# Re-cutting the HBM blocks of a streaming `x + gamma * y` kernel: 8, 60 and 60 rows instead of 4, 64 and 60

## The chip, the cores and the metric

The kernel runs on one core of a Trainium2 chip. The metric is the device time of one execution in microseconds, lower is better. Three runs of the kernel before gave 119.56, 119.86 and 119.68 us, median 119.68 us. A separate execution was profiled; its page and trace are what the rest of this document reads.

## The reference

```python
B, S, D = 1024, 16, 512          # x, y: bfloat16 [1024, 16, 512]; gamma: bfloat16 [512]
def reference(x, y, gamma):
    return x + gamma * y
```

Flattened, there are 16384 rows of 512 numbers (1024 bytes each). The core has 128 partitions, so each partition handles 128 rows. "A row" below means one such row in every partition at once: 128 x 1024 bytes, or 131072 bytes. x, y and the output have 128 rows each, 384 rows (50.33 MB) in all that must cross between HBM and the on-chip memory.

## The kernel before

Everything is written out by hand: which engine issues which transfer, which semaphore it waits for, and in which order the vector engine works. There are no loops over tiles at run time.

**Blocks.** `BLOCKS = [4, 64, 60]` cuts the 128 rows into three regions of HBM. In each region `rows_of` gives partition p one contiguous stretch of memory: 4, 64 or 60 rows of it. A transfer may cover part of one block, not parts of two.

**Transfers.** A transfer is written `(tensor, first row, end row[, slot])`; for x the slot is where it lands in `x_sb`, which holds only 76 rows, so later x loads overwrite rows of x that have been used up. y lands in `y_sb`, which holds all 128 rows; the results are written over y and stored from there. The queue of SyncE (SP) issues the list `SP`, the queue of ScalarE (ACT) issues the list `ACT`:

```python
SP  = [('y', 0, 4), ('y', 4, 68), ('x', 4, 68, 4), ('y', 68, 128), ('x', 68, 120, 24), ('x', 120, 128, 0)]
ACT = [('x', 0, 4, 0), ('g',), ('s', 4, 68), ('s', 0, 4), ('s', 68, 128)]
```

`'g'` loads gamma, `'s'` stores. In the text a transfer is called by its list entry, for instance "y 4:68" or "the store 68:128". Within one list the order is fixed, and an issuing queue that waits holds up all that is behind it.

**What holds transfers back.** `EARLY = (2, 1)` puts the first two SP transfers and the first ACT transfer ahead of the start-up barrier of the program. `HOLD = ('y', 0, 4)` with `AHEAD = (2, 1)`: the third SP transfer and the second ACT transfer wait until y 0:4 has landed; TensorE takes that semaphore and passes it on (L147, L149). `RELEASE = ('x', 68, 120, 24)`: no store is issued before that load has landed; again TensorE waits for it and passes it on, to ACT as `s_go` (L158) and to VectorE as `s_rel` (L159). An x load that overwrites rows in `x_sb` waits for the additions that read those rows (`frees`). A store waits for its additions through the counter `s_add`.

**Vector work.** `PIECES = [8, 16, 44, 52, 8]` cuts the rows for VectorE: piece 0 is rows 0:8, piece 1 is 8:24, piece 2 is 24:68, piece 3 is 68:120, piece 4 is 120:128. `('m', c)` multiplies piece c of y by gamma in place (L180), `('a', c)` adds x (L189). The order is

```python
DVE = [('m', 0), ('m', 1), ('m', 2), ('a', 2), ('a', 0), ('a', 1), ('m', 3), ('m', 4), ('a', 3), ('a', 4)]
```

Each operation waits for the loads that cover its piece. Gamma is copied to all partitions by one matmul with a row of ones (L152) and a copy out of PSUM (L154).

Of the kernel before, what the change touches and what calls it, by code (L numbers as in the profile page):

```python
# [3 lines left out]

BLOCKS = [4, 64, 60]

PIECES = [8, 16, 44, 52, 8]


SP = [
    ('y', 0, 4),
    ('y', 4, 68),
    ('x', 4, 68, 4),
    ('y', 68, 128),
    ('x', 68, 120, 24),
    ('x', 120, 128, 0),
]
ACT = [('x', 0, 4, 0), ('g',), ('s', 4, 68), ('s', 0, 4), ('s', 68, 128)]  # L20

EARLY = (2, 1)

HOLD, AHEAD = ('y', 0, 4), (2, 1)

RELEASE = ('x', 68, 120, 24)

DVE = [('m', 0), ('m', 1), ('m', 2), ('a', 2), ('a', 0), ('a', 1), ('m', 3), ('m', 4), ('a', 3), ('a', 4)]
MULT, ADD = mybir.AluOpType.mult, mybir.AluOpType.add


def _take(sem, n, eng):


    return eng.wait_ge(sem, n).then_inc(sem, -n)  # L35


def kernel(
# [18 lines left out]
    rows = N // P  # L57
    n = len(PIECES)
    assert sum(PIECES) == rows
    starts = [sum(PIECES[:c]) for c in range(n + 1)]  # L60
    dt = xf.dtype
    edges = [sum(BLOCKS[:c]) for c in range(len(BLOCKS) + 1)]
    assert edges[-1] == rows

    def rows_of(t, a, b):

        c = max(c for c in range(len(BLOCKS)) if edges[c] <= a)
        assert b <= edges[c + 1]
# [6 lines left out]
    y_sb = nc.alloc_sbuf_tensor("y_sb", [P, rows, D], dt).ap()  # L75
    x_loads = [w for w in ACT + SP if w[0] == "x"]
    y_loads = [w for w in SP + ACT if w[0] == "y"]
    stores = [w for w in SP + ACT if w[0] == "s"]
    for loads in (x_loads, y_loads, stores):
# [9 lines left out]
    s_add, s_go, s_rel, s_end, s_out = sem("s_add"), sem("s_go"), sem("s_rel"), sem("s_end"), sem("s_out")  # L89
    added = [a for kind, *a in DVE if kind == "a"]  # L90
    order = {a[0]: k for k, a in enumerate(added)}

    def meets(a, b, c, d):
        return a < d and c < b
# [4 lines left out]
    def x_at(row):  # L99
        return next(w[3] + row - w[1] for w in x_loads if w[1] <= row < w[2])  # L100
# [12 lines left out]
    def ring(eng, what, n_early, n_ahead):  # L113

        known, went = 0, False
        for k, w in enumerate(what):
            kind = w[0]
            if k == n_ahead:
                _take(s_held[eng], 1, eng)
            need = frees(w) if kind == "x" else pieces_of(w[1], w[2]) + list(w[3:]) if kind == "s" else []  # L120
            need = max((order[c] + 1 for c in need), default=0)
            if kind == "s" and not went:
                _take(s_go, 1, eng)
                went = True
            if need > known:
                eng.wait_ge(s_add, need)
                known = need
            if kind == "g":
                i = eng.dma_start(out=gamma_row, in_=gamma.unsqueeze(0)).then_inc(s_gamma, 16)
            elif kind == "x":  # L130
                to = x_sb[:, w[3] : w[3] + w[2] - w[1], :]
                i = eng.dma_start(out=to, in_=rows_of(xf, w[1], w[2])).then_inc(s_load[w], 16)
            elif kind == "y":
                r = slice(w[1], w[2])
                i = eng.dma_start(out=y_sb[:, r, :], in_=rows_of(yf, w[1], w[2])).then_inc(s_load[w], 16)
            else:
                r = slice(w[1], w[2])
                i = eng.dma_start(out=rows_of(of, w[1], w[2]), in_=y_sb[:, r, :]).then_inc(s_out, 16)
            if k < n_early:
                early.append(i.ins)  # L140

    ring(nc.sync, SP, EARLY[0], AHEAD[0])
    ring(nc.scalar, ACT, EARLY[1], AHEAD[1])

# [11 lines left out]

    _take(s_load[RELEASE], 16, nc.tensor)
    nc.tensor.sem_inc(s_go, 1)  # L158
# [4 lines left out]
    def need(loads, c):  # L163
        for w in loads:
            if w not in landed and meets(starts[c], starts[c + 1], w[1], w[2]):
                if w == RELEASE:
                    _take(s_rel, 1, nc.vector)
                elif w == HOLD:
                    _take(s_held[nc.vector], 1, nc.vector)
                else:  # L170
                    _take(s_load[w], 16, nc.vector)
                landed.add(w)

    for kind, *args in DVE:
        c = args[0]
        yt = y_sb[:, starts[c] : starts[c + 1], :]
        if kind == "m":
            need(y_loads, c)
            g = gamma_sb[:, None, :].to_broadcast([P, PIECES[c], D])
            nc.vector.tensor_tensor(out=yt, in0=yt, in1=g, op=MULT).then_inc(s_dve, 1)  # L180
            open_mults += 1
        else:
# [4 lines left out]
            at = x_at(starts[c])  # L187
            xt = x_sb[:, at : at + PIECES[c], :]
            nc.vector.tensor_tensor(out=yt, in0=xt, in1=yt, op=ADD).then_inc(s_add, 1)  # L189
# [44 lines left out]
```

## Time and profile before

| what | value |
|---|---|
| median of three runs | 119.68 us (119.56 to 119.86) |
| profiled execution, first to last instruction | 118.2 us |
| runs' median less that span | 1.5 us, lies around the span; the page gives no other time for the profiled execution |
| VectorE busy | 70.1 us (59%), 12 instructions |
| TensorE busy | 0.6 us |
| moved by DMA | 50.33 MB, mean 426 GB/s over the span |
| share of 16 DMA engines' span taken by packets | 64.8% SP's queue + 33.9% ACT's queue |

How to read it: `q1` is SP's DMA queue, `q10` is ACT's. Both feed the same 16 DMA engines. In the timeline a `DMA_DIRECT2D` row of SPq or ACTq is the issuing of a transfer, not the transfer; the list of DMA issues gives the time from issue to landing, so issue time plus that time is when the transfer's semaphore has reached its full count. The list leaves the size out where a partition's stretch is 64 rows. The profile's rows for VectorE name a tile by partitions x elements: 128x4096 is 8 rows, 128x8192 16 rows, 128x22528 44 rows, 128x26624 52 rows.

### The profile page before, as it was taken

To read this page: it belongs to the slowest core of one execution; us is meant where nothing else is said; L and a number is where in the kernel's file an instruction comes from. 1 tells how busy PE (TensorE), PEld (TensorE's weight loads), DVE (VectorE), ACT (ScalarE), POOL (GpSimd) and SP (SyncE) were. 2 spreads that over 40 slices of the span, in tenths; PEclk is the share of its full clock that TensorE was granted. 3 is DMA by queue.
4 is the path that set the end of the run, shared out by engine and by line. 5 is a ranking of instruction groups with operands and counts; after the bars stand their busy time and mean duration, and the time that the engine had idled before them with its cause. 6 is when DMAs were issued, how large, how long until landed. Compare 5 with 4: busy or idle time off the path is not lost. (4 is left out here: it accounts for less than half of the span.)

```text
span 118.2 us, 91 instructions
## 1 busy us (share of the span) xinstructions
PE 0.6 (0%) x1; PEld 0.1 (0%) x1; DVE 70.1 (59%) x12; POOL 0.2 (0%) x4
## 2 busy tenths in 40 slices
PE   0000100000000000000000000000000000000000
PEld 0000000000000000000000000000000000000000
DVE  0000200089999969999999999999999900000000
POOL 0000000000000000000000000000000000000000
DMA  6999889988899879879969696898899889799793
GB/s 248 461 666 399 355 355 399 665 355 355 355 599 466 355 333 624 374 333 499 499 288 576 288 576 288 360 637 355 355 576 488 355 355 510 333 582 416 333 499 166
DMA packets 1442, 50.33 MB, mean 426 GB/s; under 512 B 161, under 2 KB 162, under 8 KB 546
## 3 DMA queue, kind: packets, MB, share of 16 engines
q1 hardware_dynamic: 864, 33.03, 64.8%
q10 hardware_dynamic: 578, 17.30, 33.9%
HBM read 33.56 MB, written 16.78 MB: 426 GB/s over the span
## 5 line engine op out<-in xcount | busy, mean ns | idle before, releaser
L180 DVE TENSOR_TENSOR y_sb<-y_sb,gamma_sb 128x4096 bf16<-128x4096 bf16 (+3 forms) x5 | 34.7, 6981 | 10.9 <-DVEq L35 10.9
L189 DVE TENSOR_TENSOR y_sb<-x_sb,y_sb 128x4096 bf16<-128x4096 bf16 (+3 forms) x5 | 34.7, 6981 | 1.2 <-DVEq L35 1.1
L154 DVE CAST gamma_sb<-gamma_ps 128x512 bf16<-128x512 f32 x1 | 0.7, 692 | 10.2 <-DVEq L35 10.2
L146 DVE MEMSET ones_row<- 1x128 bf16 x1 | 0.2, 165 | 2.0 <-PEq L51 2.0
L152 PE MATMUL gamma_ps<-gamma_row,ones_row 1*128 1x512 bf16 x1 | 0.6, 581 | 11.6 <-PEq L35 11.6
L152 PEld LDWEIGHTS gamma_ps<-gamma_row,ones_row 1*128 1x128 bf16 x1 | 0.1, 101 | 11.6 <-issue 11.6
L218 POOL MEMSET const-bfloat16-1.0<- 128x1 bf16 x1 | 0.1, 101 | 0.0
L218 POOL MEMSET const-uint8-127<- 128x1 uint8 x1 | 0.1, 101 | 0.0
L218 POOL MEMSET const-float32-0.0<- 128x1 f32 x1 | 0.1, 98 | 0.2 <-issue 0.2
L218 POOL MEMSET const-float32-1.0<- 128x1 f32 x1 | 0.1, 98 | 0.0
## 6 DMA issues: line engine op xcount, KB each, us to landing
y_sb<-in_y_dram SPq DMA_DIRECT2D x1, 7680.0 KB, 57.3
out_dram<-y_sb ACTq DMA_DIRECT2D x1, 7680.0 KB, 23.8
x_sb<-in_x_dram SPq DMA_DIRECT2D x1, 6656.0 KB, 21.7
x_sb<-in_x_dram SPq DMA_DIRECT2D x1, 1024.0 KB, 22.0
y_sb<-in_y_dram SPq DMA_DIRECT2D x1, 512.0 KB, 3.4
x_sb<-in_x_dram ACTq DMA_DIRECT2D x1, 512.0 KB, 4.2
out_dram<-y_sb ACTq DMA_DIRECT2D x1, 512.0 KB, 22.3
y_sb<-in_y_dram SPq DMA_DIRECT2D x1, 23.4
```

Source lines behind the costliest of these rows:

```text
L146: nc.vector.memset(ones_row, 1.0).then_inc(s_ones, 1)
L152: nc.tensor.matmul(gamma_ps, ones_row, gamma_row, start=True, stop=True).then_inc(s_ps, 1)
L154: nc.vector.tensor_copy(out=gamma_sb, in_=gamma_ps).then_inc(s_dve, 1)
L180: nc.vector.tensor_tensor(out=yt, in0=yt, in1=g, op=MULT).then_inc(s_dve, 1)
L189: nc.vector.tensor_tensor(out=yt, in0=xt, in1=yt, op=ADD).then_inc(s_add, 1)
L218: nc = _bacc.Bacc("TRN2", target_bir_lowering=False, num_devices=1)
```

## The change

The blocks become 8, 60 and 60 rows. The head is the 8 rows of y alone, issued by SP; the head's 8 rows of x are the last load instead of the first. The x load 68:128 is one transfer, and piece 3 is 60 rows. ACT has no transfer ahead of the barrier; its first is gamma, behind the hold. The stores are 60, 60 and 8 rows, and the 8-row head is the last of them. The functions are unchanged.

```diff
-BLOCKS = [4, 64, 60]
-
-PIECES = [8, 16, 44, 52, 8]
+BLOCKS = [8, 60, 60]
+
+PIECES = [8, 16, 44, 60]
 
 
 SP = [
-    ('y', 0, 4),
-    ('y', 4, 68),
-    ('x', 4, 68, 4),
+    ('y', 0, 8),
+    ('y', 8, 68),
+    ('x', 8, 68, 0),
     ('y', 68, 128),
-    ('x', 68, 120, 24),
-    ('x', 120, 128, 0),
+    ('x', 68, 128, 16),
+    ('x', 0, 8, 0),
 ]
-ACT = [('x', 0, 4, 0), ('g',), ('s', 4, 68), ('s', 0, 4), ('s', 68, 128)]
-
-EARLY = (2, 1)
-
-HOLD, AHEAD = ('y', 0, 4), (2, 1)
-
-RELEASE = ('x', 68, 120, 24)
-
-DVE = [('m', 0), ('m', 1), ('m', 2), ('a', 2), ('a', 0), ('a', 1), ('m', 3), ('m', 4), ('a', 3), ('a', 4)]
+ACT = [('g',), ('s', 8, 68), ('s', 68, 128), ('s', 0, 8)]
+
+EARLY = (2, 0)
+
+HOLD, AHEAD = ('y', 0, 8), (2, 0)
+
+RELEASE = ('x', 68, 128, 16)
+
+DVE = [('m', 0), ('m', 1), ('m', 2), ('a', 2), ('a', 1), ('m', 3), ('a', 3), ('a', 0)]
```

## The prediction

> **What bounds the kernel now.** I read the page from the top. VectorE is busy 59% of the span, no other engine counts, and the chain of waits accounts for only 14% of the span, since it does not follow transfers. The queues account for the rest:
>
> ```profile
> ## 3 DMA queue, kind: packets, MB, share of 16 engines
> q1 hardware_dynamic: 864, 33.03, 64.8%
> q10 hardware_dynamic: 578, 17.30, 33.9%
> HBM read 33.56 MB, written 16.78 MB: 426 GB/s over the span
> ```
>
> 64.8% and 33.9% make 98.7%: of 118.2 us the sixteen DMA engines lack packets for 1.5 us. So the question is whether the transfers stand end to end. The DMA issues give the time to landing, the timeline the issue:
>
> ```profile
> y_sb<-in_y_dram SPq DMA_DIRECT2D x1, 7680.0 KB, 57.3
> out_dram<-y_sb ACTq DMA_DIRECT2D x1, 7680.0 KB, 23.8
> x_sb<-in_x_dram SPq DMA_DIRECT2D x1, 6656.0 KB, 21.7
> x_sb<-in_x_dram SPq DMA_DIRECT2D x1, 1024.0 KB, 22.0
> y_sb<-in_y_dram SPq DMA_DIRECT2D x1, 512.0 KB, 3.4
> x_sb<-in_x_dram ACTq DMA_DIRECT2D x1, 512.0 KB, 4.2
> out_dram<-y_sb ACTq DMA_DIRECT2D x1, 512.0 KB, 22.3
> y_sb<-in_y_dram SPq DMA_DIRECT2D x1, 23.4
> x_sb<-in_x_dram SPq DMA_DIRECT2D x1, 39.5
> ...
> out_dram<-y_sb ACTq DMA_DIRECT2D x1, 21.5
> ```
>
> ```profile
> 0.00 0.85 SPq L135 DMA_DIRECT2D y_sb<-in_y_dram  x2
> ...
> 3.71 0.33 SPq L132 DMA_DIRECT2D x_sb<-in_x_dram  x1
> 3.90 0.50 ACTq L129 DMA_DIRECT2D gamma_row<-in_gamma_dram  x1
> 4.09 0.43 SPq L135 DMA_DIRECT2D y_sb<-in_y_dram  x1
> ...
> 55.37 2.53 SPq L132 DMA_DIRECT2D x_sb<-in_x_dram  x2
> ...
> 77.41 17.36 ACTq L138 DMA_DIRECT2D out_dram<-y_sb  x3
> ```
>
> Rows merged here ("x2", "x3") start, singly, at 0.00 and 0.42; 55.37 and 57.58; 77.41, 77.81 and 94.43. Issue plus time to landing: y 0:4 at 3.4, x 0:4 at 4.3, y 4:68 at 0.42 + 23.4 = 23.8, x 4:68 at 43.2, y 68:128 at 61.4, x 68:120 at 77.1, x 120:128 at 79.6, stores at 98.9, 100.1 and 118.2. The steps are 19.4 us for 64 rows, 18.2 for 60, 15.7 for 52, 2.5 for 8, then 19.3, 1.2 and 18.1 for 64, 4 and 60 rows stored: 0.302 to 0.303 us a row in all the wide ones, loads and stores, and the narrow ones the same within rounding. Each step is the transfer's own bytes; none holds a pause. In the trace's packet records every engine starts the next transfer's first packet within 0.05 us of its last one of the transfer before. So no transfer waits for VectorE; I check below that this stays so.
>
> **The row transfers.** The bytes are the same: 384 rows. Ten row transfers become nine: y 0:4, x 0:4, y 64, x 64, y 60, x 52, x 8, and stores 64, 4, 60 give way to y 8, y 60, x 60, y 60, x 60, x 8, and stores 60, 60, 8. A transfer is 8 packets on each engine, one per partition. Their durations by size are 2.418 us (65536 bytes), 2.267 (61440), 0.309 (8192) and 0.159 (4096). From the two ends, (2.418 - 0.159) / 61440 bytes = 36.8 ns per 1000 bytes, which leaves 0.159 - 0.151 = 0.008 us a packet. One transfer fewer saves 8 x 0.008 = 0.06 us. Above, I can bound the cost of a transfer by stores 4 and 60 together, 1.2 + 18.1 = 19.3 us, against 19.3 us for the one of 64 rows: with 0.1 us rounding, 0 to 0.15. I take 0.07, the packet value; range 0 to -0.2 (the upper bound plus the slow first packets of the cold start: y 0:4 took 1.36 us an engine where the store of 4 rows took 1.27).
>
> Here the Trainium skill points elsewhere. "DMA: Bandwidth & Descriptors", section "Anatomy of one DMA", fits a fixed 2.0 us per DMA plus the bytes (for GpSimd's path); by it one transfer fewer would give about 117.7 us. The same page, "Measured (HBM→SBUF, 128 partitions, SWDGE, issued from GpSimd)", gives 6.15 us to a single 1 MB transfer, which speaks against an 8-row store at the very end: counted at 6.15 instead of 2.5 it would give about 123.3 us. The rows above decide: a 1 MB load queued behind another took 2.5 us and a half-MB store 1.2 us.
>
> **The head.** Before, two queues filled the first 8 rows; now one does. Engines start at 1.00 us, as y 0:4 did. Eight packets of 0.309 us last to about 3.5, where y 8:68 must be ready. It is issued at 0.42, like y 4:68. The nearest row is x 0:4, issued at 0.13 and moving at 2.21, so at most 2.1 us: ready by 2.5. The loosest bound is y 4:68 itself, whose first packet came at 3.65, behind others: at worst a pause of 3.65 - 3.5 = 0.15 us. I take 0.
>
> y 0:8 lands when x 0:4 did, 4.3 instead of 3.4, so what the hold releases is 0.9 us later: x 8:68 about 4.6, y 68:128 about 5.0, and gamma about 4.8. The x load is needed at 22.3, so that is free. Gamma moved at 8.62 (behind two 64-row packets) and TensorE had it at 11.5; a later issue makes it 12.4, or, with one packet more in front, 2.3 us later still, 14.7. Matmul to end of copy was 1.5 us. The multiplication of rows 8:24 needs it at 22.6. Piece 0's multiplication, 2.29 us, no longer waits for y 4:68 and fits in between.
>
> **The middle.** At 0.303 us a row: y 8:68 lands at 23.8 - 4 x 0.303 = 22.6 (68 rows loaded instead of 72), x 8:68 at 40.8, y 68:128 at 59.0, x 68:128 at 77.1 and x 0:8 at 79.6 (248 and 256 rows, as before). VectorE: pieces 1 and 2 multiplied from 22.7 take 4.42 + 11.89, to 39.0, before x lands. Additions of pieces 2 and 1 from 41.0 to 52.9 and 57.3. The first frees slots 16:60 of `x_sb`, so x 68:128 goes out at 53.0; it must move at 58.7: a cover of 5.7 us, as before (55.37 against 61.0). The second frees slots 0:8, and x 0:8 goes out at 57.4, needed at 76.7.
>
> A 60-row operation isn't in the trace. From 44 and 52 rows, 11.89 and 14.02, 0.267 us a row, so 14.02 + 8 x 0.267 = 16.15. Piece 3's multiplication: 59.1 to 75.3, before 77.1. Deleting one multiplication and one addition saves VectorE little, since the rows remain; nothing on the path.
>
> **The stores.** Released by the same landing at 77.1, with the same 8-row load as cover: before, landing to issue took 0.35 us, and issue to first packet 1.32 us at most (77.41 to 78.73); no engine was idle. The structure is unchanged, so 0. The issue of the store 8:68 waits for additions done at 57.3.
>
> The store 68:128 is new in second place: it waits for the addition of all 60 rows. 77.6 + 16.15 = 93.75, issued at 93.8; ready by 95.1 with the same 1.32. The store 8:68 keeps the engines until about 96.9 (s 4:68 ended, first engine, at 98.1, less 1.2 for four rows). Cover 1.8 us; before, 94.43 + 1.32 = 95.75 against 99.29, 3.5 us. The last addition, 2.29 us, ends at 96.0, and the store 0:8 is issued at 96.1 and moves at 115. The 0.35 us from last packet to landing (117.84 to 118.19) stays; 8-row x took 0.37.
>
> **Sum.** The profiled span is 118.2 us; the runs' median 119.68 is 1.5 above, and I take that to stay. 118.2 - 0.07 + 0 + 0 + 0 = 118.1, or 119.68 - 0.07 = 119.6 us.
>
> **The rivals.** *Fewer, larger transfers gain more than the rows say.* 384 rows at the pure byte rate (36.8 ns per 1000 bytes, 50.33 MB over 16 engines) take 115.7 us of the 116.85 between first packet (1.00) and last (117.84). Everything that packets and starts cost is therefore 1.2 us, of which the change touches a tenth (one transfer of ten) and the cold head: at most 0.3, 119.35 us. Beyond 0.3% only with the runs' own scatter (0.25% between the three) on its side. For it: fewer packets; against: pauses between transfers read as nothing.
>
> *Slower: the store 68:128 comes too late.* Place: between the 60-row stores. From 1.8 us of lateness on, each further microsecond is paid in full; 60-row addition 10% slower beside stores (1.6 us) would still be free, 15% (2.4) would cost 0.6 and give 120.2. Against it: the 52-row addition ran beside stores at 14.02 us, and the multiplication, beside loads, also at 14.02. A store whose start takes 2 us more than the first one's would give about 119.8, three more 120.8.
>
> *The release pauses.* If the store 8:68 became ready 0.5 us later than 4:68 did, up to 0.5 would be lost: 120.1. No row suggests it.
>
> *It doesn't do what it says* (blocks of 8 rows slowing the partition stretches): 8192-byte packets took 0.309 us and 60-row ones 2.267, each at the common rate. With 3% on the three 8-row transfers: 0.2 us, 119.8.
>
> **How the numbers follow.** A difference under about 0.3%, 0.36 us, is what a measurement of this kernel cannot tell from none. Forecast, no visible change: 0.72. Larger gain: 0.13. Late second store: 0.07; paused release: 0.05; a slow 8-row block or head that costs more than its bounds: 0.03. Faster 0.13, same 0.72, slower 0.15. The range runs from 119.2 (the larger gain with scatter) to 120.1 (a paused release, a mildly late store).
>
> **What would show it.** Right: the steps between landings stay at 0.303 us a row, y 8:68 near 22.6, x 8:68 near 40.8, y 68:128 near 59.0, x 68:128 near 77.1, stores at about 97.7, 115.8 and 118.2; queue shares again sum to about 98.7%; 60-row operations at 16.15. Wrong: a step longer than its rows, above all from y 0:8 to y 8:68 (18.3 expected), from x 0:8 to the first store (18.1), or between the stores; a store 68:128 issued after 95.6; or a changed gap between span and run time.

## The result, and the profile after

The change makes the kernel slightly slower. 21 runs of each in turn gave 119.94 us (119.79 to 120.17) after and 119.72 us (119.56 to 119.94) before, a ratio of 1.0018, 95% interval 1.0012 to 1.0024. That is 0.22 us, inside the 0.3% that I called "no visible change", but with that many runs clear of zero and on the other side of the 0.07 us gain that I had summed. Two later measurements of the same two kernels gave 1.0010 and 1.0009 (e12 and e14 below), so the loss is 0.1 to 0.2 us.

The profiled execution of after spans 118.7 us (118.66 by its records; before 118.23). The queues of after:

```profile
q1 hardware_dynamic: 864, 33.55, 65.8%
q10 hardware_dynamic: 434, 16.78, 32.7%
```

98.5% instead of 98.7%: still a kernel of transfers end to end. The DMA issues of after (each with its size and the time from issue to landing) and the issue times in its timeline:

```profile
y_sb<-in_y_dram SPq DMA_DIRECT2D x1, 7680.0 KB, 22.6
y_sb<-in_y_dram SPq DMA_DIRECT2D x1, 1024.0 KB, 4.8
...
x_sb<-in_x_dram SPq DMA_DIRECT2D x1, 7680.0 KB, 36.0
y_sb<-in_y_dram SPq DMA_DIRECT2D x1, 7680.0 KB, 53.8
...
x_sb<-in_x_dram SPq DMA_DIRECT2D x1, 7680.0 KB, 24.1
x_sb<-in_x_dram SPq DMA_DIRECT2D x1, 1024.0 KB, 22.3
...
out_dram<-y_sb ACTq DMA_DIRECT2D x2, 7680.0 KB, 21.1
out_dram<-y_sb ACTq DMA_DIRECT2D x1, 1024.0 KB, 22.1
```

```profile
0.00 0.85 SPq L135 DMA_DIRECT2D y_sb<-in_y_dram  x2
...
5.17 0.33 SPq L132 DMA_DIRECT2D x_sb<-in_x_dram  x1
5.37 0.52 ACTq L129 DMA_DIRECT2D gamma_row<-in_gamma_dram  x1
5.55 0.43 SPq L135 DMA_DIRECT2D y_sb<-in_y_dram  x1
...
53.36 4.66 SPq L132 DMA_DIRECT2D x_sb<-in_x_dram  x2
...
77.84 19.02 ACTq L138 DMA_DIRECT2D out_dram<-y_sb  x3
```

Rows merged here start, singly, at 0.00 and 0.42; 53.36 and 57.69; 77.84, 94.32 and 96.53. Issue plus time to landing: y 0:8 at 4.8, y 8:68 at 23.0, x 8:68 at 41.2, y 68:128 at 59.4, x 68:128 at 77.5, x 0:8 at 80.0, the stores at 98.1, 116.2 and 118.6. The steps behind the head are 18.2, 18.2, 18.2, 18.1, 2.5, 18.1, 18.1 and 2.4 us: their rows at 0.303 us, within 0.1 us. Only the first number, the landing of the head, is off. Eight rows had landed at 4.34 us before (x 0:4) and land at 4.84 us after. From there to the last landing it is 118.19 - 4.34 = 113.85 us before and 118.63 - 4.84 = 113.79 after. So in these two executions the head loses 0.50 us, and the rest gains 0.06.

Answers of the stage view, for the same stretches before and after, show it (columns: stretch, its length, busy time of PE, PEld, DVE and POOL, granted clock, DMA share, GB/s; a packet is booked whole where it starts). Before:

```profile
0.80:2.00 1.20, 0.00 (x0) 0.00 (x0) 0.01 (x1) 0.00 (x0) 1.00 0.79 294
...
1.10:1.50 0.40, 0.00 (x0) 0.00 (x0) 0.00 (x0) 0.00 (x0) 1.00 0.81 287
```

After:

```profile
0.80:2.00 1.20, 0.00 (x0) 0.00 (x0) 0.01 (x1) 0.00 (x0) 1.00 0.72 137
...
1.10:1.50 0.40, 0.00 (x0) 0.00 (x0) 0.00 (x0) 0.00 (x0) 1.00 0.00 0
```

In both, the first packet starts at 1.00 us. In the packet records of before, the first ten 4096-byte packets take 0.18 to 0.35 us where 0.159 is usual. In after, four of the first 8192-byte packets take 1.22 to 1.31 us where 0.309 is usual, and many of the next 0.4 to 0.8. Summed over the head's packets, the time beyond the usual is 0.11 us an engine before and 0.48 after; in the transfer behind, 0.14 and 0.04. That is the first loss; the second is a late start. After, eight packets start up to 1.08 us and no other before 1.51, so eight of the sixteen engines have moved nothing by then; between 1.2 and 1.6 us, 13.7 engines are at work on average before, 8.1 after. From 1.0 to 2.5 us an engine is without a packet for 0.15 us on average before and for 0.34 after. The two losses, 0.37 and 0.19 us an engine, make up the 0.50, roughly.

The times are medians of many runs; the profiles are one execution each, and the two spans differ by 0.44 us where the medians differ by 0.22. After's profiled execution took 119.99 us, 1.33 more than its span. In all 17 profiled executions whose time is known, after and e1 to e16, this gap is 1.32 or 1.33 us. With 1.33 around before's span of 118.23, that execution took 119.56 us, the lowest of its 21 runs. If all of the scatter lies in the head, a median execution has it near 4.5 before and near 4.8 after (an estimate from the medians, the gap and the times above), and the head's loss is 0.3 us rather than 0.50. Two later profiles of after had the head at 4.74 and 4.72.

### The profile page after: what moved, and what is told of

Its sections match the earlier page's. It is cut to its first block, busy times and chain, and to the rows that moved or that the text cites. A ratio compares the mean times of both kernels' runs of the same rounds, so it can differ in the third digit from the quotient of the medians.

```text
span 118.7 us, 87 instructions
## 1 busy us (share of the span) xinstructions
PE 0.6 (0%) x1; PEld 0.1 (0%) x1; DVE 70.1 (59%) x10; POOL 0.2 (0%) x4
## 5 line engine op out<-in xcount | busy, mean ns | idle before, releaser
L189 DVE TENSOR_TENSOR y_sb<-x_sb,y_sb 128x22528 bf16<-128x22528 bf16 (+3 forms) x4 | 34.6, 8688 | 4.5 <-DVEq L35 4.5
## 6 DMA issues: line engine op xcount, KB each, us to landing
x_sb<-in_x_dram SPq DMA_DIRECT2D x1, 1024.0 KB, 22.3
```

## The experiments

All ratios are to the kernel before, run in turn with them, with 95% intervals. "Head landed" is the landing of the first 8 rows, or of the first transfer, in the one profiled execution. Each kernel also gives the time from the head's landing to the end, and with after's transfers it hardly moves: in the three profiles of after and in e13 and e15 it is 113.69 to 113.79 us, in e1 113.93 and in e5 114.06; e7 is the exception, with 115.58. So, e7 apart, the head's landing time tells most of a run's time.

### First question: packet size, the missing second queue, or the place in HBM?

Each theory explains the slow first packets: 8192-byte packets instead of 4096; one queue at the head instead of two; or neighbouring partitions' stretches 8192 bytes apart.

**e1**: after, with the head cut in two.

```diff
-    ('y', 0, 8),
+    ('y', 0, 4),
+    ('y', 4, 8),
-EARLY = (2, 0)
+EARLY = (3, 0)
-HOLD, AHEAD = ('y', 0, 8), (2, 0)
+HOLD, AHEAD = ('y', 4, 8), (3, 0)
```

> The kernel after with its 8-row head cut into y 0:4 and y 4:8, both on SP; everything else, the block of 8 rows in HBM included, as after. Theory (the first packets at a cold start stall, and the stall grows with the packet's size, 8192 bytes against 4096): the head's 8 rows land at about 4.3 to 4.4 us instead of 4.8, y 8:68 and all behind it 0.4 us earlier, time about 119.7 us, ratio to before 0.999 to 1.001. Rival (the head has lost its second queue): 8 rows land at 4.8 as in the kernel after, time 119.95 us, ratio 1.002. Rival (the 8-row block's layout in HBM is slow when cold): also 4.8 and 1.002.

Measured: 120.79 us, ratio 1.0086 (1.0071 to 1.0100). Half the packet size made it worse by more than the whole change had; the first four rows, 4096-byte packets, landed at 3.9 (before 3.4), all eight at 5.5. Small packets alone do not cure the start, against my theory; none of the three had said 120.8.

**e2**: before, with x 0:4 moved from ACT's head to SP behind x 4:68, so that the head has one queue.

```diff
     ('x', 4, 68, 4),
+    ('x', 0, 4, 0),
-ACT = [('x', 0, 4, 0), ('g',), ...
+ACT = [('g',), ...
-EARLY = (2, 1)
+EARLY = (2, 0)
-HOLD, AHEAD = ('y', 0, 4), (2, 1)
+HOLD, AHEAD = ('y', 0, 4), (2, 0)
```

> The kernel before with x 0:4 taken from ACT's head and issued by SP right behind x 4:68; blocks 4, 64 and 60 as before. Theory (packet size): y 0:4 lands at 3.4 us as before and y 4:68 at 22.6 (four rows fewer in front); time as before, ratio 0.999 to 1.001. Rival (second queue): y 0:4 or the first packets of y 4:68 come some 0.4 us late, y 4:68 at 23.0, ratio 1.002 to 1.004. Note that 65536-byte packets come second here, so a slow start of those would show in this run too.

Measured: 119.80 us, ratio 1.0004 (0.9993 to 1.0016). The DMA issues of this run, the first two transfers:

```profile
y_sb<-in_y_dram SPq DMA_DIRECT2D x1, 512.0 KB, 3.3
y_sb<-in_y_dram SPq DMA_DIRECT2D x1, 22.3
```

3.3 as before (3.4), and y 4:68 at 0.42 + 22.3 = 22.7: no pause behind the head. A 4-row head does not need the second queue.

**e3**: before, with blocks of 8, 60 and 60 and a head of y 0:8 on SP and x 0:8 on ACT.

```diff
-BLOCKS = [4, 64, 60]
+BLOCKS = [8, 60, 60]
-    ('y', 0, 4),
-    ('y', 4, 68),
-    ('x', 4, 68, 4),
+    ('y', 0, 8),
+    ('y', 8, 68),
+    ('x', 8, 68, 8),
-ACT = [('x', 0, 4, 0), ('g',), ('s', 4, 68), ('s', 0, 4), ('s', 68, 128)]
+ACT = [('x', 0, 8, 0), ('g',), ('s', 8, 68), ('s', 0, 8), ('s', 68, 128)]
-HOLD, AHEAD = ('y', 0, 4), (2, 1)
+HOLD, AHEAD = ('y', 0, 8), (2, 1)
```

> The kernel before with blocks of 8, 60 and 60 rows, and a head of y 0:8 on SP and x 0:8 on ACT: the two queues of before with the packet size of after. Theory (packet size): the first packets take 0.5 to 1.3 us, y 0:8 lands near 4.8 or a little earlier, time about 119.9, ratio 1.002. Rival (second queue): no stall, y 0:8 lands at 4.3, time 119.7, ratio 1.000.

Measured: 120.00 us, ratio 1.0019 (1.0010 to 1.0028), the loss of the change with before's two queues. With e2 this rules the queue out from both sides: one queue with a 4-row head loses nothing, two queues with an 8-row head do. (y 0:8 landed at 6.4 here, because the two 8-row transfers and y 8:68 took turns; the landing cannot be compared. Its first packets took up to 1.16 us.)

**e4**: after, with a head of 16 rows (blocks 16, 56, 56).

```diff
-BLOCKS = [8, 60, 60]
+BLOCKS = [16, 56, 56]
-PIECES = [8, 16, 44, 60]
+PIECES = [16, 20, 36, 56]
...
-    ('x', 68, 128, 16),
-    ('x', 0, 8, 0),
+    ('x', 72, 128, 20),
+    ('x', 0, 16, 0),
```

> The kernel after with a head of 16 rows, blocks 16, 56 and 56 (16384-byte packets at the head, last load and last store of 16 rows). Theory (stall grows with the packet): the engines start moving steadily another 0.3 to 0.6 us later than in the kernel after; time 120.2 to 120.5, ratio 1.004 to 1.007. Rival (a fixed cold cost of a one-queue head): as the kernel after, 119.95, ratio 1.002.

Measured: 121.07 us, ratio 1.0113 (1.0095 to 1.0131), above the expected range. Not all of it is the head: y 0:16 landed at 7.8, where 16 rows at 0.303 from 1.00 plus 0.35 would be 6.2, an estimate (by which after's 8 rows would have landed at 3.8 instead of 4.8, and before's at 3.8 instead of 4.3); the last load, x 0:16, lost another 0.6 us an engine around the time the first store was issued.

### Second question: the distance of the stretches, with all else equal

**e5**: after with one line changed.

```diff
-BLOCKS = [8, 60, 60]
+BLOCKS = [68, 60]
```

> The kernel after with HBM blocks of 68 and 60 rows instead of 8, 60 and 60. The transfers, their order and their packet sizes (8192 bytes at the head) are those of the kernel after; only the distance in HBM between the stretches of neighbouring partitions changes, from 8192 to 69632 bytes for the head and from 61440 to 69632 for rows 8:68. Theory now (the head stalls because sixteen engines start together on stretches 8192 bytes apart): no stall, the first transfer moves at over 280 GB/s between 0.8 and 2.0 us as in the kernel before (293; after 137), y 0:8 lands near 4.2, time 119.6 to 119.75, ratio 0.999 to 1.0005. Rival (size of the first packets): stall as after, 8 rows at 4.8, ratio 1.002. Rival (issue of the 60-row transfer right behind the head): as after, 1.002.

Measured: 119.77 us, ratio 1.0004 (0.9996 to 1.0013), head landed at 4.5. Taken alone it supported the distance as the cause; see e13.

**e6**: e1 with its head in two blocks; x and the stores of the head are then in two transfers as well.

```diff
-BLOCKS = [8, 60, 60]
+BLOCKS = [4, 4, 60, 60]
-    ('x', 0, 8, 0),
+    ('x', 0, 4, 0),
+    ('x', 4, 8, 4),
-ACT = [('g',), ('s', 8, 68), ('s', 68, 128), ('s', 0, 8)]
+ACT = [('g',), ('s', 8, 68), ('s', 68, 128), ('s', 0, 4), ('s', 4, 8)]
```

> Blocks of 4, 4, 60 and 60 rows: the head is y 0:4 and y 4:8 as in the run with a 4 and 4 head, but each now lies in a block of its own (stretches 4096 bytes apart, as at the head of before). x 0:4 and x 4:8 are the last loads, the stores of 0:4 and 4:8 the last stores. Theory (distance of the stretches): the head does not stall, 8 rows land near 4.3, time 119.7 to 119.9 with two transfers more than after (0.06 us each), ratio 1.000 to 1.001. Rival (three transfers issued ahead of the barrier on one queue are what cost 0.85 us in that run): 120.8, ratio 1.008.

Measured: 120.69 us, ratio 1.0080 (1.0063 to 1.0098). The head is what the theory said, the total is not. DMA issues of e1 and e6, the two 4-row transfers (median of two). e1:

```profile
y_sb<-in_y_dram SPq DMA_DIRECT2D x2, 512.0 KB, 4.5
```

e6:

```profile
y_sb<-in_y_dram SPq DMA_DIRECT2D x2, 512.0 KB, 3.7
```

Four-row stretches side by side land 0.8 us sooner than the same stretches 8192 bytes apart (8 rows at 4.5 against 5.5). But y 8:68, issued third at 0.88, then landed 1.0 us later than 60 rows should (23.7 against 4.5 + 18.2): two of its first packets took 3.03 and 3.07 us where 2.27 is usual, and one of these was the last to start, at 4.42 us.

**e7**: after, with y 8:68 issued behind the barrier.

```diff
-EARLY = (2, 0)
+EARLY = (1, 0)
```

> The kernel after with only y 0:8 issued ahead of the start-up barrier; y 8:68 is issued behind it at about 1.9 us. Theory (distance of the stretches): the head stalls as in after, 8 rows at 4.8, ratio 1.002, or more if y 8:68 is not ready in time. Rival (issuing the 60-row transfer disturbs the head's first packets): no stall, 8 rows at 4.3, ratio 0.999 to 1.001.

Measured: 121.56 us, ratio 1.0140 (1.0109 to 1.0172), far above the range. The DMA issue of y 8:68, which in this run begins at 1.42 us:

```profile
y_sb<-in_y_dram SPq DMA_DIRECT2D x1, 7680.0 KB, 23.5
```

1.42 + 23.5 = 24.9, against 23.0 in after. The head itself landed at 4.9, as in after, so its slow packets are not caused by the issue of the transfer behind it. That transfer's first packets started between 3.85 and 6.27 us on the sixteen engines, the last 4.8 us after the issue, though all of the head was done at 4.5.

**e8**: after, with a head of 12 rows; its transfers follow.

```diff
-BLOCKS = [8, 60, 60]
+BLOCKS = [12, 56, 60]
-PIECES = [8, 16, 44, 60]
+PIECES = [12, 16, 40, 60]
```

> Blocks of 12, 56 and 60 rows, otherwise as after: head of 12 rows in stretches of 12288 bytes, 12288 apart; last load and last store of 12 rows. Theory (distance of the stretches, and powers of two worst): the head runs nearly free, time 119.6 to 119.8, ratio 0.999 to 1.001, although its packets are larger than the 8192 bytes of after. Rival (size of the first packets): the stall lies between that of the heads of 8 and 16 rows, time 120.2 to 120.8, ratio 1.004 to 1.009.

Measured: 120.70 us, ratio 1.0081 (1.0066 to 1.0097): between heads of 8 and 16 rows, so a distance that is no power of two did not help. y 0:12 landed at 6.2 (5.0 by the estimate as in e4). The last load lost 0.2 us an engine here as well.

**e9 and e10** differ in `BLOCKS` alone. Both are after with

```diff
-    ('y', 0, 8),
+    ('y', 0, 4),
-    ('x', 0, 8, 0),
+    ('x', 0, 4, 0),
+    ('x', 4, 8, 4),
-ACT = [('g',), ('s', 8, 68), ('s', 68, 128), ('s', 0, 8)]
+ACT = [('y', 4, 8), ('g',), ('s', 8, 68), ('s', 68, 128), ('s', 0, 4), ('s', 4, 8)]
-EARLY = (2, 0)
+EARLY = (2, 1)
-HOLD, AHEAD = ('y', 0, 8), (2, 0)
+HOLD, AHEAD = ('y', 0, 4), (2, 1)
```

and e9 alone also with

```diff
-BLOCKS = [8, 60, 60]
+BLOCKS = [4, 4, 60, 60]
```

> The kernel after with a head of y 0:4 on SP and y 4:8 on ACT, each in a block of its own (blocks 4, 4, 60, 60), the hold on y 0:4; x 0:4 and x 4:8 the last loads, the stores 0:4 and 4:8 the last stores. Only BLOCKS differs from its partner with blocks of 8, 60 and 60. Theory (compact 8-row block is slow at a cold start because of where its stretches lie): clean head, over 200 GB/s between 0.8 and 2.0 us, time within 0.1 us of before, ratio 0.999 to 1.001. Rival (only the packet size matters): the same as its partner, both near 1.000. Rival (y 8:68 behind the head is what comes late): both at 1.002 or more.

> As its partner with blocks 4, 4, 60, 60, but the head's two 4-row transfers lie in one block of 8 rows, so that the stretches of neighbouring partitions are 8192 bytes apart and not 4096; packets of 4096 bytes, queues and order the same. Theory (where the stretches lie): the head stalls as in the kernel after, under 200 GB/s between 0.8 and 2.0 us, ratio 1.002 to 1.004. Rival (packet size): clean, 1.000.

Measured: e9 119.97 us, ratio 1.0014 (1.0002 to 1.0026); e10 120.92 us, ratio 1.0097 (1.0083 to 1.0112). DMA issues, e9:

```profile
y_sb<-in_y_dram SPq DMA_DIRECT2D x1, 512.0 KB, 4.0
y_sb<-in_y_dram ACTq DMA_DIRECT2D x1, 512.0 KB, 4.8
```

e10:

```profile
y_sb<-in_y_dram SPq DMA_DIRECT2D x1, 512.0 KB, 4.7
y_sb<-in_y_dram ACTq DMA_DIRECT2D x1, 512.0 KB, 5.5
```

0.95 us between the medians of kernels whose transfers, packet sizes, queues and order are the same. In the two profiled executions it is 0.7 (spans of 118.8 and 119.5 us), and all of it is there when the head lands. Where the head's stretches lie matters at the start. e9 has twelve row transfers, three more than after; from the landing of its 8 rows to the end it took 113.86 us, about 0.1 more than after. Its profiled execution had y 0:4 at 4.0, later than the 3.3 of e2 and e6; its first packet started at 1.12 us, not at 1.00, and why, I can't say.

**e11**: e4 with its blocks changed; **e12**: after once more, without an edit.

```diff
-BLOCKS = [16, 56, 56]
+BLOCKS = [72, 56]
```

> The run with a head of 16 rows (121.07 us) with blocks of 72 and 56 rows instead of 16, 56 and 56: packets, order and sizes as there, the head's stretches 73728 bytes apart instead of 16384. Theory (where the stretches lie): most of that run's loss goes, ratio 1.000 to 1.004. Rival (packet size at the head and in the last load): stays at 1.010 to 1.013.

> The kernel after once more, beside the others on the same chip: 119.9 to 120.0 us, ratio 1.001 to 1.003, the head's 8 rows landing at 4.7 to 4.9 us and the first transfers moving at 120 to 160 GB/s between 0.8 and 2.0 us.

Measured: e11 120.93 us, ratio 1.0096 (1.0083 to 1.0109), so moving the 16-row stretches apart takes away little: y 0:16 landed at 7.3 instead of 7.8, but the last load lost 1.0 us an engine instead of 0.6. e12 119.89 us, ratio 1.0010 (1.0001 to 1.0018).

**e13 to e16** set e5 and after side by side on one chip, and vary the distance in both kernels. e13 is e5 again, e14 is after again. e15 is after with

```diff
-BLOCKS = [8, 60, 60]
+BLOCKS = [128]
```

and e16 is before with

```diff
-BLOCKS = [4, 64, 60]
+BLOCKS = [68, 60]
```

> The kernel after with blocks 68 and 60, a second time, in one call with the kernel after itself. Theory (the distance of the head's stretches is the cause): 0.1 to 0.25 us below the kernel after of the same call, ratio to before 0.9995 to 1.001, head landed at 4.5 to 4.6 us. Rival (8-row packets on one queue are the cause): level with the kernel after, 1.001 to 1.002, head at 4.75 to 4.85.

> The kernel after, in one call with its partner of blocks 68 and 60: 119.85 to 120.0 us, ratio 1.001 to 1.002, head landed at 4.75 to 4.85 us.

> The kernel after with one block of 128 rows: all stretches 131072 bytes apart, transfers and packet sizes those of after. Theory (8192 bytes apart is what hurts the head): head as with 68 rows, landed at 4.5 to 4.6 us, ratio 0.9995 to 1.001, unless the power-of-two distance slows the bulk too, which would show as steps longer than 18.2 us per 60 rows. Rival (8-row packets): 1.001 to 1.002 with the head at 4.8.

> The kernel before with blocks of 68 and 60 rows instead of 4, 64 and 60; nothing else changed. The 4-row packets of its head then come from stretches 69632 bytes apart instead of 4096. Theory (8192 bytes apart is the bad case, farther apart is not): head and time as before, y 0:4 at 3.4, x 0:4 at 4.3, ratio 0.999 to 1.001. Rival (4096 bytes apart, close together, is a good case of its own): head later by some 0.3 us, ratio 1.002 to 1.004.

Measured: e13 119.92 us, 1.0012 (1.0003 to 1.0021); e14 119.88 us, 1.0009 (1.0000 to 1.0018); e15 119.94 us, 1.0016 (1.0008 to 1.0025); e16 119.96 us, 1.0015 (1.0007 to 1.0024). DMA issues, the head of e13:

```profile
y_sb<-in_y_dram SPq DMA_DIRECT2D x1, 1024.0 KB, 4.9
```

and of e16, the kernel before with nothing changed but the blocks:

```profile
y_sb<-in_y_dram SPq DMA_DIRECT2D x1, 512.0 KB, 3.9
x_sb<-in_x_dram ACTq DMA_DIRECT2D x1, 512.0 KB, 4.8
```

e13 takes back what e5 seemed to show: e5's one profile apart, an 8-row head lands at 4.7 to 4.9 whether its stretches are 8192, 69632 or 131072 bytes apart. e5 and e13 are one kernel; their ratios, 1.0004 and 1.0012, have overlapping intervals, and their profiled heads, 4.5 and 4.9, show how far single executions differ. e16 shows the other half: before's own 4-row head loses its lead (3.9 and 4.9 instead of 3.4 and 4.3), and the kernel loses as much as by the whole change, when its stretches no longer lie side by side.

**What follows.** Shown: the change's loss lies in the head, in slow first packets and in engines that start late. A 4-row head needs no second queue (e2), and a second queue doesn't avoid the loss of an 8-row head (e3). The loss is not due to the issue of the transfer behind the head (e7), and not simply to the distance of 8192 bytes (e13, e15). The distance does change how the start is slow. In all three profiles of after, no packet starts between 1.1 and 1.5 us, and the head's packets then take 0.35 to 0.48 us an engine beyond the usual. With stretches 69632 or 131072 bytes apart (e13, e15, e16) the same 0.4 us move 123 to 205 GB/s, but the first transfer's packets take 0.60 to 0.62 us an engine beyond the usual, and the time is no better.

The good start is that of 4-row, 4096-byte stretches lying side by side, half a megabyte in one piece (before, e2, e6; e9's profile, with such stretches too, was slower). Small packets alone are not enough (e1, e10, e16), and stretches side by side alone are not either (after). Either step away, stretches of 8 rows (after, e3, e13, e15) or the same 4 rows spread out (e16; worst at 8192 bytes, e1 and e10), costs 0.1 to 1.1 us; e5 alone, with 1.0004, shows no clear loss.

Open: what in the memory or the DMA engines makes it so. For heads that lie side by side, packet size and the extent of the first transfer could not be told apart, since a smaller packet in one piece is also a smaller extent. Open too is the scatter of single executions: the same 4-row head took 0.09 us an engine beyond the usual in before and 0.25 in e2, and landed at 3.4 and 3.3. No kernel tried was faster than before.

## Why the prediction was wrong

**The step that failed** is the head, "I take 0", with "at worst a pause of 3.65 - 3.5 = 0.15 us" as its loosest bound, and "y 0:8 lands when x 0:4 did, 4.3". It landed at 4.84, and at 4.74 and 4.72 in the two later profiles of after. In place of the 0 the runs showed a cold start that costs 0.3 us by the medians (the estimate above) and 0.50 between the two profiles: half of the engines begin after 1.5 us, and the first packets are slow. I bounded only whether the next transfer would be ready when the head ended. I did not ask how long the head's own packets take on engines that have moved nothing yet, and gave the eight of them the 0.309 us of a running transfer (x 120:128). The only cold row of the trace, y 0:4, showed 0.09 us an engine beyond the usual, and I used that as part of a gain. It was the row of another shape, and the runs show that shape and place decide: 0.48 us for the 8 rows of after, 0.60 for the same 4 rows spread out (e16). A cold 8-row transfer was not in the trace and should have been bounded like any unseen operation: with the excess of y 0:4's first packets scaled up as one end, and the range wider on the slow side.

**The readiness bound** in the same step, "at most 2.1 us" from issue to first packet, came out harmless here but does not hold elsewhere: in e7 the last engine took 4.8 us, with nothing else left to do since 4.5 us into the program. In after, y 8:68 was issued at 0.42 and no engine waited for it.

**The transfer saved** was forecast at 0.07 us. The 0.06 between the two profiles agrees, but is not clear of the scatter: e16, with before's ten row transfers, took 113.73 us from the landing of its 8 rows to the end, no more than after's nine (113.72 to 113.79). Step by step, e9's two 4-row loads at the end took 2.52 us where after's one of 8 rows took 2.47, and its two 4-row stores 2.43, the same as after's one. So a transfer more costs 0 to 0.05 us there. The Trainium skill's fixed 2.0 us per DMA ("DMA: Bandwidth & Descriptors", "Anatomy of one DMA", for GpSimd's path) does not describe a transfer queued behind another here, and neither do the 6.15 us that its "Measured (HBM→SBUF, 128 partitions, SWDGE, issued from GpSimd)" gives for 1 MB: the 8-row load at the end took 2.5, the 8-row store 2.4.

**The middle** was right in its steps and covers, every time about 0.4 us later because of the head. A 60-row operation was put at 16.15 us. By shape, after's VectorE shows

```profile
L180 DVE TENSOR_TENSOR y_sb<-y_sb,gamma_sb 128x30720 bf16<-128x30720 bf16 x1 | 16.2, 16158 | 1.8 <-DVEq L35 1.8
L189 DVE TENSOR_TENSOR y_sb<-x_sb,y_sb 128x30720 bf16<-128x30720 bf16 x1 | 16.2, 16158 | 2.5 <-DVEq L35 2.5
```

16.158 us, and idle time in front of each: VectorE waits for loads, no transfer for VectorE. Gamma reached TensorE at 13.5 (12.4 to 14.7 forecast).

**The stores** were right. The first was issued 0.35 us after the landing it waits for and moved without a pause; the store 68:128 was issued at 94.3 (93.8 forecast) and moved at 97.1, so with the 1.32 us of before from issue to first packet it came 1.5 us early, and the rival in which it comes too late did not occur. The other slower rival, the paused release, did not occur either; nor did 8-row stretches slow down once engines were running (x 0:8 took 2.5 us). The rival of a slow head was given 0.03 of chance together with the slow 8-row block.

**The base of the sum** held a lucky execution. I took 1.5 us around the span by setting before's profiled span against the median; after's own execution shows 1.33. The 4.3 us of the head that I carried over belonged to one of before's fastest executions, so of the 0.50 us between the two profiles some 0.2 is the luck of that execution (an estimate, as above).

**The numbers.** 119.94 us lies in the range 119.2 to 120.1 and within 0.3% of before; the sign is wrong and the forecast of 119.6 is 0.3 us too low, which is the head. That it lies in the range is no merit of the sum: the slow side of the range was there for a paused release and a late store, and neither occurred.

## What to carry to other kernels

In this kernel, whose transfers stand end to end, steady rows priced everything in the change but the first transfer; larger loads placed last (below) were the other exception among the runs. What the head lost was paid in full at the end, so look at the first packets in the records, and price a new head by a cold row of its own shape or leave it open. Keep the first transfer as small and as contiguous as it was when it started well, and issue the second one before the engines run out of the first.

## What the runs showed of the hardware that I had not expected

The engines that start late stay late. The spread of landing times over the sixteen engines is set in the first microseconds and kept to the end: 0.47 us at after's head and 0.56 at its last store; 0.28 and 0.43 before; 1.0 and 0.8 in e10; 1.9 at y 8:68 in e7, where it fell to 0.85 only at the stores, whose release had waited for the last engine: the 8-row load that covers the release ends sooner on the engines that are ahead. This wait cost e7 nothing that shows at the end. Its time from the head to the end grew to 115.58 us from 113.8, but all of that is the step to y 8:68, 20.0 us instead of 18.2; the steps behind it are those of after within 0.04 us.

A transfer issued 1.42 us into the program took up to 4.8 us to start moving (e7), when the store issued at 77.4 in before had its first packet after 1.32 and the last engine's after 1.76, with the engines busy until then. Loads of 12 and 16 rows placed last lost 0.2 to 1.0 us an engine beside the first store's issue (e8, e4, e11), where those of 8 rows lost 0.1 at most; no run shows why.
